# A recurrent-memory attention kernel: one output pass for regular and left rows, and attention scores in 12 products per head group with K's shared chunk in two half-zero planes

## The chip, the cores and the metric

The kernel runs on one core of a Trainium2 chip. The metric is the device time of one execution in microseconds (us); lower is better. Engine names as in the profile: PE is TensorE's matrix products and PEld its weight loads, DVE is VectorE, ACT is ScalarE, POOL is GpSimd, SP is the engine that issues most of the data transfers (DMAs).

## The reference, cut to what matters

```python
# B, S, Dm = 1, 2048, 640; H, Dh = 32, 192; M = 8 memory rows, seg_len = 32; Df = 1536; all bfloat16
mem = mem0
for s in range(S // seg_len):                    # 64 segments, one after the other
    h = concat([mem, x[s]])                      # 8 + 32 = 40 rows
    q, k, v = h @ Wq, h @ Wk, h @ Wv             # 32 heads of 192
    scores = where(mask, q @ k.T * Dh**-0.5, -1e9)
    o = (softmax(scores) @ v) @ Wo               # 40 x 640
    mem = o[:8]                                  # memory for the next segment
    outs.append(o[8:])
a = concat(outs)
b = (gelu(x @ w_gate) * (x @ w_up)) @ w_down
g = sigmoid((x * gate_w).sum(-1))
return g * a + (1 - g) * b
```

The next segment needs the 8 memory rows of this one, so the attention part is a chain of 64 steps.

## The kernel before

**Parts.** A feed-forward part comes first (the b branch, the gate, and x in a transposed form kept in DRAM). Then come 64 segments. A tile of 32 columns takes the 8 memory rows and the first 24 rows of x; they are called the regular rows. The last 8 rows of x are the left rows. Their Q, K and V do not depend on the memory, so these are computed for four segments at a time (4 x 8 = 32 rows, `left_mm`); Q and K of them are kept in DRAM as `left_qk_scratch`; they are read back into a stage and copied beside the regular columns by `left_fill`. q is the segment number modulo 4.

**Weights.** All weights together do not fit into SBUF. A piece is the [128, 1536] slice of Wq, Wk or Wv for 8 heads and one of five slices of Dm (384 KB), or a pair of heads of Wo (480 KB). Thirteen of the first and three of the second kind share their place with another piece: in every segment these 16 are replaced once used (`swap_loads`, `load_piece`, line 599, issued by SP in order), and are used again in the same segment for the last octet. An octet is 8 heads; a segment has four, and odd segments go through them backwards.

**Order of work.** `PROG` is a list written out by hand that gives the order of the items within a segment for all engines. `("g", n, k)` is slice k of a group of projections (`GROUPS`, up to three of Q, K, V sharing a stationary operand: lines 1046 and 226, 32-column tiles, four at once); `tq` and `tk` are the DVE transposes of Q and K (line 1080); `sc` the scores, `ex` the softmax, `pt` the transposed probabilities (lines 1144 and 1149), `pv` the products with V (lines 1177 and 1179), `wo` the products with Wo, two items per octet, `lf` and `le` products and read-out of the left Q and K (line 884, 891), `vb` V of the next left rows. There are seven groups: the last three are K of octet 3 behind V and Q, and V of octet 3 alone. Each engine takes its instructions in the order in which they are added; waits are set from the regions that an operation reads and writes.

**Scores (line 1083).** Scores of an octet go into one PSUM bank: two heads in the columns and four pairs. A head has 192 features, so a pair of heads has three chunks of 128: one of each head, and a middle one that holds 64 features of each. A mask product opens the bank (line 1087, two products), then eight products with all 128 rows (line 1095), then eight with 64 rows each for the middle chunk (line 1100, upper and lower half of the array). DVE then takes the maximum (1112) and subtracts it (1114), ACT the exponential (1124), DVE sum, reciprocal and the two products (1126 to 1131). Q and K, transposed, stand in `Qs` and `Ks`, 12 chunks of 40 columns.

**Products with V and Wo.** `pv_oct` writes the 40 columns per chunk and pair; ACT copies them into one of two buffers `uT` (line 1188; for octet 3 the third chunk is copied by DVE, line 1193). POOL copies the 8 left columns into `uTl` (line 1196), which gathers four segments. The 32 regular columns are multiplied by Wo at once: octets 0 to 2 in `wo_split` (line 1206, two head pairs side by side, four 32-column tiles of 320) with two halves that have to be added (`half_sums`: an ACT copy, line 1212, and two DVE sums, line 1215), octet 3 into a bank of its own (line 1229, 160 wide). The results are summed (line 1371) and transposed (line 1375) into the memory columns of the next segment; this is the boundary. In q3, `wo_left` takes the 32 gathered left rows through the same Wo pieces (also line 1206), behind each of the regular items and, for the last item, behind the boundary; `left_sums` adds their halves at the start of the next q0, after the first scores, reading bank 4.

**Small transfers.** Per four segments, `bzl_load` (line 952) reads the left rows of b in four DMAs and `outl_store` (line 961) writes the finished rows in four; both are issued by SP, the first in q2, the second in q0. The queue of SP is one list too: weight pieces, stages, the loads of b and the stores stand in program order.

Of the kernel before, what the change touches and what calls it, by code (L numbers as in the profile page):

```python
# [230 lines left out]

def _build(nc, A_x, A_mem0, A_Wq, A_Wk, A_Wv, A_Wo, seg_len, w_gate, w_up, w_down,
# [46 lines left out]
    total = int(nc.sbuf_bytes_remaining) - 64  # L279
# [5 lines left out]
    wsA = {}  # L285
    wsB = {}
    wsA["XB"] = al(DJ * 2)
    wsA["xs"] = al(KT * XA * 2)
    wsA["gall"] = al(NSEG * 4)
    wsA["gallL"] = al(32 * 4)  # L290
    wsA["ident"] = al(128 * 2)
    wsA["maskm"] = al(R * 2)
    wsA["elw"] = al(2 * 7 * 16 * 2)
    wsA["XLg"] = 2 * al(KT * 32 * 2)
    NVB, NUB = 2, 2
    wsB["bzl"] = al(DJ * 2)
    wsB["K"] = al(12 * R * 2)
# [5 lines left out]
    wsB["uT"] = al(NUB * 12 * R * 2)  # L303
    wsB["stats"] = al(2 * 3 * 4 * 4 + 8)
    wsB["p"] = al(4 * 64 * 2)
    wsB["uTl"] = al(NCH * 32 * 2)
# [63 lines left out]
    gallL = fview(wsA_off["gallL"], 128)  # L370
    r_gallL = sreg(wsA_off["gallL"], 128)
# [5 lines left out]
    elw = bview(wsA_off["elw"], 448).rearrange("p (i b r) -> p i b r", i=2, r=16)  # L377
    r_elw = sreg(wsA_off["elw"], 448)
# [5 lines left out]
    Ks = bview(wsB_off["K"], 12 * R * 2).rearrange("p (s r) -> p s r", r=R)  # L384
    r_Km = sreg(wsB_off["K"], 8)
    r_Kl = sreg(wsB_off["K"] + 8, 12 * R * 2 - 8)
    rows_sb = [bview(wsB_off["rows"] + b * 768, 768) for b in range(2)]
    r_rows = [sreg(wsB_off["rows"] + b * 768, 768) for b in range(2)]
    stg_off = (wsB_off["stg"], wsB_off["uT"] + 24 * R)
    assert 8 * LW <= 24 * R  # L390
# [23 lines left out]
    r_uTp = [[sreg(wsB_off["uT"] + b * UB, 4), sreg(wsB_off["uT"] + b * UB + 4, 4)] for b in range(NUB)]  # L414
    st_f = [[fview(wsB_off["stats"] + (3 * b + i) * 16, 16) for i in range(3)] for b in range(2)]
    r_st = [sreg(wsB_off["stats"] + 48 * b, 48) for b in range(2)]
    uTl = bview(wsB_off["uTl"], NCH * 64).rearrange("p (c t) -> p c t", t=32)
    r_uTl = [sreg(wsB_off["uTl"] + 12 * 64 * b, 12 * 64) for b in range(NOCT)]
    bz, bzl = [bview(wsB_off[nm], DJ * 2) for nm in ("bz", "bzl")]
    Zt = PT[:, 0:DJ]  # L420
    r_bzlj = [sreg(wsB_off["bzl"], DJ * 2, 32 * j, 32 * j + 32) for j in range(4)]
# [8 lines left out]
    fp_sz = {"xst": 16 * KT * XA * 2, "xls": 4 * KT * 64, "gr": 512 + 4 * NSEG + 128, "gwT": 64}  # L430
# [13 lines left out]
    r_gin = [sreg(o_gr + 512, 4 * NSEG, 32 * j, 32 * j + 32) for j in range(4)]  # L444
# [46 lines left out]
    def piece_src(key):  # L491
        if key[0] == 3:
            return Wo2[:, key[1]]
        m, o_, k = key
        return (Wq2, Wk2, Wv2)[m][:, k, OW * o_:OW * (o_ + 1)]
# [975 lines left out]
```

## Time and profile before

| what | value |
|---|---|
| runs of the kernel | 1756.74, 1765.19, 3865.19 us; median 1765.19 |
| span of the profiled execution | 1765.1 us |
| PE busy | 92% of the span |
| PEld, DVE, ACT, POOL busy | 46%, 54%, 45%, 18% |
| DMA engines busy with the main queue | 78.3% |
| moved | 499.57 MB, 283 GB/s on average |
| mean granted TensorE clock | 0.994 |
| start of segment 1 (first transpose of line 1375) | 204.3 us |

The profiled execution took 1765.1 us from its first to its last instruction, the median of the runs. Times in the profile are in us unless marked ns. A row with "x" and a count is a group of instructions; two numbers "start, us" in a timeline are the start and the length of a merged stretch, so what a product costs in a stream is read from one start to the next. In a list of waits the first name waited for the second. "issue" as the releaser means that the profile shows nothing that the engine waited for.

### The profile page before, as it was taken

The page shows a single profiled execution, that of the slowest core. Times are in us where ns is not written, and L with a number is a line of the kernel's source. Part 1 is how long each engine was busy: PE and PEld are TensorE (multiplying, and loading weights), DVE is VectorE, ACT ScalarE, POOL GpSimd, SP SyncE. Part 2 cuts the span into 40 slices and gives each one's busy share as a digit, 9 for nine tenths or more (in the row PEclk, how much of TensorE's full clock was granted, in tenths as well). Part 3 has the DMA queues.
Part 4 walks back from the last instruction along what each step waited for, and adds up shares of the span by engine and source line. Part 5 has one row for each costly group of instructions (what it writes and reads, how often), then busy time and mean ns, then how long its engine had stood idle before and what let it go on. Part 6 is the DMA issues. An engine that isn't in the chain of part 4 may idle for free.

```text
span 1765.1 us, 80301 instructions
## 1 busy us (share of the span) xinstructions
PE 1623.9 (92%) x39162; PEld 809.5 (46%) x31501; DVE 960.0 (54%) x2932; ACT 802.8 (45%) x1835; POOL 320.0 (18%) x1099
## 2 busy tenths in 40 slices
PE   9999999999999999999999989999999998999887
PEld 4554444444444444454444444454444444454444
DVE  2222655556555655555555655555555655655554
ACT  3222544545444544444444544444444544445443
POOL 1100111111112112111212111111211121121211
PEclk9999999999999999999999999999999999999999
DMA  9814987888778887888788887879787886879776
GB/s 335 295 48 157 329 313 250 320 313 288 280 269 311 299 308 253 315 290 319 281 280 293 296 293 250 314 285 323 279 280 275 311 310 241 312 282 327 283 275 238
DMA packets 271311, 499.57 MB, mean 283 GB/s; under 512 B 105304, under 2 KB 132208, under 8 KB 270960
## 3 DMA queue, kind: packets, MB, share of 16 engines
q1 hardware_dynamic: 267832, 491.34, 78.3%
q8 instruction: 276, 4.52, 1.0%
q10 hardware_dynamic: 3128, 3.09, 0.6%
q14 instruction: 75, 0.61, 0.1%
HBM read 473.22 MB, written 21.11 MB: 280 GB/s over the span
## 4 chain that ended last, share of the span: by engine, by line
PE 71%; DVE 15%; DMA 6%; issue 4%; ACT 4%; DVEq 0%; SPq 0%; ACTq 0%
PE ps L1046 20%; PE ps L226 15%; PE ps L1206 8%; DMA arena<-in_A_Wo_dram 5%; PE ps L1177 3%; PE ps L804 3%; PE ps L801 3%; PE ps L884 3%; PE ps L1100 3%; PE ps L819 2%; PE ps L1087 2%; DVE ps L1114 2%; DVE arena L1112 2%; PE ps L1095 2%; PE ps L1229 2%
## 5 line engine op out<-in xcount | busy, mean ns | idle before, releaser
L1046 PE MATMUL ps<-arena 128*32 128x384 bf16 x9940 | 723.0, 329 | 42.4 <-DVE arena L1375 34.4
L226 PE MATMUL ps<-arena 128*32 128x384 bf16 x7680 | 595.4, 328 | 7.9 <-DVE arena L1215 3.5
L1046 PEld LDWEIGHTS ps<-arena 128*32 128x32 bf16 x9940 | 257.5, 97 | 365.3 <-issue 226.0
L1080 DVE STREAM_TRANSPOSE arena<-arena 128x384 bf16<-128x384 bf16 x512 | 270.8, 557 | 150.8 <-ACT arena L1066 149.2
L1066 ACT ACTIVATE arena<-ps 128x384 bf16<-128x384 f32 x512 | 236.2, 489 | 211.6 <-PE ps L1046 196.3
L1206 PE MATMUL ps<-arena 128*32 128x320 bf16 x6144 | 293.6, 301 | 13.9 <-issue 13.4
L1124 ACT ACTIVATE ps<-ps 104x160 f32<-104x160 f32 x256 | 71.9, 281 | 293.4 <-DVE ps L1114 293.4
L1206 PEld LDWEIGHTS ps<-arena 128*32 128x32 bf16 x6144 | 163.5, 97 | 74.0 <-issue 19.4
L1112 DVE TENSOR_REDUCE arena<-ps 104x4 f32<-104x160 f32 x256 | 83.0, 324 | 165.8 <-PE ps L1100 164.6
L941 POOL COPY arena<-arena 128x96 bf16<-128x96 bf16 x256 | 70.3, 275 | 513.4 <-PE ps L1100 444.2
L1188 ACT ACTIVATE arena<-ps 128x480 bf16<-128x480 f32 (+1 forms) x256 | 137.0, 535 | 43.8 <-PE ps L1179 39.6
L1196 POOL COPY arena<-arena 128x96 bf16<-128x96 bf16 x256 | 68.3, 267 | 441.1 <-ACT arena L1188 357.3
L1162 ACT ACTIVATE arena<-ps 128x448 bf16<-128x448 f32 x192 | 104.2, 543 | 96.7 <-PE ps L1149 96.4
L1069 ACT ACTIVATE arena<-ps 128x384 bf16<-128x384 f32 x256 | 125.1, 489 | 20.9 <-PE ps L1046 16.3
L1177 PE MATMUL ps<-arena 128*64 128x160 bf16 x1536 | 123.1, 243 | 12.5 <-ACT arena L1162 6.9
L1126 DVE TENSOR_REDUCE arena<-ps 104x4 f32<-104x160 f32 x256 | 83.0, 324 | 92.5 <-ACT ps L1124 92.5
L1177 PEld LDWEIGHTS ps<-arena 128*64 128x64 bf16 x1536 | 80.8, 109 | 91.6 <-issue 31.7
L884 PE MATMUL ps<-arena 128*32 128x384 bf16 x1280 | 111.4, 330 | 2.2 <-issue 2.0
L1179 PE MATMUL ps<-arena 128*64 128x64 bf16 x1536 | 104.8, 193 | 4.1 <-issue 4.1
L891 DVE STREAM_TRANSPOSE arena<-arena 128x384 bf16<-128x384 bf16 x128 | 73.7, 576 | 31.6 <-ACT arena L889 27.8
L1215 DVE TENSOR_TENSOR arena<-ps,arena 64x160 f32<-64x160 f32 x160 | 50.8, 317 | 72.3 <-ACT arena L1212 61.6
L1114 DVE TENSOR_TENSOR ps<-ps,arena 104x160 f32<-104x160 f32 x256 | 85.0, 332 | 8.8
(84 smaller groups left out, 1819.2 us busy)
## 6 DMA issues: line engine op xcount, KB each, us to landing
arena<-in_A_Wk_dram SPq DMA_DIRECT2D x335, 384.0 KB, 7.1
arena<-in_A_Wv_dram SPq DMA_DIRECT2D x335, 384.0 KB, 9.1
arena<-in_A_Wo_dram SPq DMA_DIRECT2D x205, 480.0 KB, 6.4
arena<-in_A_Wq_dram SPq DMA_DIRECT2D x209, 384.0 KB, 5.4
arena<-left_qk_scratch SPq DMA_DIRECT2D x126, 96.0 KB, 2.8
left_qk_scratch<-arena SPq DMA_DIRECT2D x49, 192.0 KB, 2.3
left_qk_scratch<-arena SPq DMA_DIRECT2D x30, 96.0 KB, 5.7
ffn_b_scratch<-arena ACTq DMA_DIRECT2D x16, 160.0 KB, 4.4
```

The source lines that it names most:

```text
L226: return e.add_instruction(mybir.InstMatmult(name=nm, start_tensor_calc=like["start"], stop_tensor_calc=stop, tile_size=(128, 32), tile_po ...
L884: fns.append(lambda e, outp=outp, rhs=rhs, j=j: e.matmul(outp, lhs, rhs, start=(k == 0), stop=(k == KT - 1), tile_position=(0, 32 * j)))
L1046: fns.append(lambda e, outp=outp, rhs=rhs, j=j: e.matmul(outp, lhs, rhs, start=(k == 0), stop=(k == KT - 1), tile_position=(0, 32 * j)))
L1066: S_.add("act", lambda e, m=m, bk=bk: e.activation(out=rows_sb[m], in_=ps[:, bk, 0:384], func=ACTF.Copy), reads=[r_ps[bk]], writes=[r_rows ...
L1069: S_.add("act", lambda e, i=i, bk=bk: e.activation(out=v_sb[i % NVB].rearrange("p (c n) -> p c n", c=3), in_=ps[:, bk, 0:384].rearrange("p ...
L1080: S_.add("dve", lambda e: e.transpose(out=dst[:, :, 0:L], in_=rows_sb[m].rearrange("p (c r) -> p c r", r=L)), reads=[r_rows[m]], writes=[r ...
L1112: S_.add("dve", lambda e: e.tensor_reduce(out=mxs, in_=S3, axis=AX.X, op=ALU.max), reads=[rb], writes=[rst], name="smax max")
L1114: S_.add("dve", lambda e: e.tensor_tensor(out=S3, in0=S3, in1=mxb, op=ALU.subtract), reads=[rb, rst], writes=[rb], name="smax sub")
L1177: return [lambda e: e.matmul(full, v[:, e0:e0 + 64], PTm[:, i], start=True, stop=False, tile_position=(0, 64 * i), skip_group_check=True), ...
L1179: lambda e: e.matmul(part, vl[:, e0:e0 + 64], PTl[:, i], start=False, stop=True, tile_position=(0, 64 * i), skip_group_check=True)]
L1188: S_.add("act", lambda e: e.activation(out=apx(u[:, 0, 0, :], [[R, na], [3 * R, 4], [1, R]]), in_=ps[:, A, 0:na * W].rearrange("p (c t r) ...
L1206: fns.append(lambda e, i=i, t=t, j=j, gv=gv: e.matmul(ps[32 * j:32 * j + 32, bank, 0:2 * DJ].rearrange("p (h n) -> p h n", h=2), lhs2[i], ...
```

## The change

1. **Scores in 12 products.** K's two outer chunks go to one buffer (`KSA`). The middle chunk goes to two planes of another (`KSB`): the upper 64 rows into plane 0, the lower 64 into plane 1, and the other half of each plane is zero, set once. One product of all 128 rows and 80 columns then gives both heads of a pair: eight outer products and four middle ones (`score_mm`, `scores_mid`, item `sd`). K's DVE transpose becomes three: 128x256 and two of 64x128; POOL's copy of the left K becomes three likewise (`KPART`). Heads are paired anew (head h with h + 4), so V's products read two runs of 192 columns, and a Wo piece is put together from two heads' 64 rows.
2. **The joined output pass.** In q3 the octet's `uT` buffer is one of 64 columns (`U3`): 40 from the products with V, 24 from `uTl` by POOL. `wo_both` multiplies all 64 by a Wo piece, two products of 320 columns per chunk, into bank 4. `wo_left` is gone. The regular 32 rows are read out by two DVE and two ACT copies of 32x160 before the boundary's transposes; the left ones by four DVE operations in `left_sums`, with no halves to add.
3. **Order.** Six groups in place of seven, K before Q; `PROG` is written anew for q0 to q2 and `PROG3` for q3. The ACT copy of the half sums stays behind the last `wo` of octet 2; the DVE sums move behind the last `pv`.
4. **Small transfers.** The left rows are kept in the order of the new buffer (the fourth segment's first), so `bzl_load` and `outl_store` issue eight DMAs in place of four. Buffers in SBUF are packed anew to make room.

```diff
-    GROUPS = [[(0, 0), (1, 0)], [(2, 0), (0, 1), (1, 1)], [(2, 1), (0, 2)], [(1, 2)], [(2, 2), (0, 3)], [(1, 3)], [(2, 3)]]
+    GROUPS = [[(1, 0), (0, 0)], [(1, 1), (0, 1), (2, 0)], [(1, 2), (0, 2), (2, 1)], [(0, 3), (2, 2)], [(1, 3)], [(2, 3)]]
...
+    PROG = [("g", 0, 0), ("g", 0, 1), ("g", 0, 2), ("g", 0, 3), ("g", 0, 4), ("g", 1, 0), ("tk", 0), ("tq", 0),
+            ("g", 1, 1), ("g", 1, 2), ("sc", 0), ("sd", 0), ("g", 1, 3), ("ex", 0), ("g", 1, 4), ("g", 2, 0),
+            ("g", 2, 1), ("tk", 1), ("g", 2, 2), ("pt", 0), ("g", 2, 3), ("tq", 1), ("g", 2, 4), ("sc", 1),
+            ("sd", 1), ("lf", 2, 1, 0), ("pv", 0), ("g", 3, 0), ("g", 3, 1), ("tq", 2), ("g", 3, 2), ("lf", 1, 0, 0),
+            ("ex", 1), ("lf", 1, 0, 1), ("g", 3, 3), ("lf", 2, 1, 1), ("pt", 1), ("tk", 2), ("g", 3, 4), ("sc", 2),
...
+            ("lf", 0, 1, 2), ("pv", 3), ("lf", 1, 1, 4), ("le", 1, 1, 0), ("lf", 0, 1, 3), ("lf", 0, 1, 4),
+            ("le", 2, 1, 0), ("le", 2, 1, 1), ("le", 0, 1, 0), ("le", 1, 1, 1), ("wo", 3, 0), ("le", 0, 1, 1),
+            ("wo", 3, 1)]
+    PROG3 = [("g", 0, 0), ("g", 0, 1), ("g", 0, 2), ("g", 0, 3), ("g", 0, 4), ("tq", 0), ("g", 1, 0), ("g", 1, 1),
+            ("g", 1, 2), ("tk", 0), ("g", 1, 3), ("g", 1, 4), ("sc", 0), ("sd", 0), ("tk", 1), ("tq", 1), ("ex", 0),
...
+            ("g", 4, 3), ("tq", 3), ("g", 4, 4), ("wo", 0, 1), ("pv", 1), ("g", 5, 0), ("pt", 2), ("tk", 3),
+            ("sc", 3), ("sd", 3), ("wo", 1, 0), ("ex", 3), ("wo", 1, 1), ("pv", 2), ("g", 5, 1), ("g", 5, 2),
+            ("pt", 3), ("g", 5, 3), ("wo", 2, 0), ("g", 5, 4), ("wo", 2, 1), ("pv", 3), ("vb", 0), ("vb", 1),
+            ("vb", 2), ("wo", 3, 0), ("wo", 3, 1), ("vb", 3), ("vb", 4)]
...
+        for lo, hi, dst, cs, n in KPART:
+            S_.add("dve", lambda e, lo=lo, hi=hi, dst=dst, cs=cs: e.transpose(
+                out=dst[lo:hi, :, :, 0:L], in_=kparts(rows_sb[1], cs, L)[lo:hi]),
+                reads=[r_rows[1]], writes=[r_Km[n]], name="Tk%s s%d o%d" % ("b" if n else "", s, o))
...
-        for tl in range(4):
-            for gp in (0, 64):
-                fns.append(lambda e, gp=gp, c=3 * tl + 1, tl=tl: e.matmul(
-                    ps[gp:gp + R, bank, SC + tl * R:SC + (tl + 1) * R], Qs[gp:gp + 64, c, :], Ks[gp:gp + 64, c, :], start=False,
-                    stop=True, tile_position=(gp, gp), skip_group_check=True))
...
+        lo = SC + 2 * R * (t % 2) + (R if c == 2 else 0)
+        rhs, n = (KSB[:, t], 2) if c == 1 else (KSA[:, t, c // 2:c // 2 + 1], 1)
+        return lambda e: e.matmul(
+            ps[64 * (t // 2):64 * (t // 2) + R, bank, lo:lo + n * R].rearrange("p (x r) -> p x r", r=R), Qs[:, 3 * t + c, :], rhs,
+            start=False, stop=c == 1, tile_position=(0, 64 * (t // 2)), skip_group_check=True)
...
+    def wo_both(s, item):
+        for p in wo_pairs(s, item):
+            g_, rg_ = piece(s, (3, p))
             for c in range(3):
+                S_.add("pe", [lambda e, i=i, g_=g_, c=c, p=p: e.matmul(
+                    ps[64 * i:64 * i + 64, LB, 0:2 * DJ], U3[:, p % 4, c, :], g_[:, c, 2 * DJ * i:2 * DJ * (i + 1)],
+                    start=(p == NWP - 1 and c == 0), stop=(p == 0 and c == 2), tile_position=(0, 64 * i),
+                    skip_group_check=True) for i in range(2)],
+                    reads=[rg_, r_U3], writes=[r_ps[LB]], name="Wb s%d p%d" % (s, p))
...
+        if q == 3:
+            for j in (0, 2, 1, 3):
+                dst, src = Zt[32 * j:32 * j + 32], ps[64 * (j // 2):64 * (j // 2) + 32, LB, DJ * (j % 2):DJ * (j % 2 + 1)]
...
+            for n, (lo, hi) in enumerate(LROW):
+                S_.add(AUXQ, lambda e, j=j, n=n, lo=lo, hi=hi: e.dma_start(
+                    bzl[32 * j + M * n:32 * j + M * (n + hi - lo)], rows(b_scr, g)[1][lo:hi, :, DJ * j:DJ * (j + 1)]),
+                    reads=[Rg("dr", 128 * g, 128 * g + 128)], writes=[r_bzlj[j][n]], dma_sem="bzl%d" % (2 * j + n), name="bzl load g%d" % g)
```

## The prediction

> **What bounds the kernel now.** I read the page first.
> ```profile
> span 1765.1 us, 80301 instructions
> ...
> PE 1623.9 (92%) x39162; PEld 809.5 (46%) x31501; DVE 960.0 (54%) x2932; ACT 802.8 (45%) x1835; POOL 320.0 (18%) x1099
> ...
> q1 hardware_dynamic: 267832, 491.34, 78.3%
> q8 instruction: 276, 4.52, 1.0%
> ```
> TensorE is busy 92% of the span, and the weight stream keeps the DMA engines busy for 78%: two limits close together. The rest is asked by segment. The transposes of line 1375 hand the memory on, so I count a segment from the first of such a pair to the next. Segment 0 starts at 204 us after the feed-forward part, and 63 more follow. Let q be the number modulo 4. Mean lengths are q0 25.0, q1 25.0, q2 23.4, q3 25.3 us: 98.7 us per four, 15.75 fours. One four, by windows (busy us and instruction counts of PE, PEld, DVE, ACT, POOL, then clock, DMA share, GB/s; rows q1, q2, q3, q0):
> ```profile
> 601.65:626.92 25.27, 23.02 (x596) 10.84 (x452) 15.00 (x46) 12.28 (x29) 4.48 (x16) 1.00 0.88 306
> 626.92:650.46 23.54, 21.59 (x556) 10.19 (x432) 13.51 (x44) 11.54 (x27) 4.49 (x16) 1.00 0.87 303
> 650.46:674.55 24.09, 23.16 (x632) 12.38 (x528) 12.48 (x42) 11.07 (x26) 5.41 (x18) 1.00 0.79 291
> 674.55:699.90 25.35, 23.26 (x616) 11.80 (x492) 16.26 (x50) 12.18 (x28) 4.55 (x16) 1.00 0.78 274
> ```
> The two limits differ by segment: q1 and q2 run DMA at 0.87 to 0.88. A 384 KB weight piece lands every 0.97 us once the stream runs, a Wo piece every 1.2 us. The first piece is issued 0.85 us into a segment (1.9 us in q1) and lands at about 4.8 (q1: 5.9); the last Wo piece lands at 24.5, 22.3, 21.3 and 23.2 us in these four. From there some 0.8 us remain to the next segment (twelve products 0.4, sum and latency 0.4). So the weights alone ask for about 25.3, 23.1, 22.1 and 24.0 us. q2 stands 0.3 us above that, q3 3 us.
>
> What PE waits for (us in total, times, longest):
> ```profile
> PE ps L1046 <- DVE arena L1375: 34.4, 48, 1.2
> PE ps L1144 <- DVE arena L1131: 25.0, 65, 0.7
> PE ps L1206 <- issue: 13.4, 14, 2.0
> PE ps L1177 <- ACT arena L1162: 6.9, 15, 0.5
> PE ps L1229 <- DMA arena<-in_A_Wo_dram: 6.1, 10, 2.3
> ```
> The segment boundary costs about 0.7 us at 48 of 63 (after a q3 the late Wo pass hides it, 0.1). "Issue" waits sum to 35.6 us over all PE lines, 1.36 us per q3: up to 2 us in the middle of a group, where the instruction stream is densest. 4.52 MB over 276 fetches is 16 KB or 256 PE instructions each, so I read them as instruction fetch.
>
> **The scores.** PE's timeline of one head group:
> ```profile
> 1002.02 0.34 PE L226 MATMUL ps<-arena 128*32 128x384 bf16 x4
> 1002.28 0.25 PE L1087 MATMUL ps<-arena 128*40 128x160 bf16 x2
> 1002.37 0.26 PE L1095 MATMUL ps<-arena 128*40 128x40 bf16 x8
> 1002.56 0.27 PE L1100 MATMUL ps<-arena 64*40 64x40 bf16 x8
> 1002.76 0.35 PE L884 MATMUL ps<-arena 128*32 128x384 bf16 x4
> ```
> The starts are what count. Four 384-wide products take 0.16 us, yet 0.26 passes before the mask: 0.10 for entering the 64-column arrangement. Leaving costs the same (V's products: 0.12 to the next start, where a pair takes 0.03). Inside, L1095 to L1100 is 0.11 where a pair takes 0.03: again a change. The Trainium skill, TensorEngine Tiling (Array Packing), Key Properties, says that changing the mode, not just the tile, drains the engine. The trace agrees, at 0.08 to 0.10 us.
>
> Mask to exit is now 0.48 us. After: 0.09 mask, 0.11 for eight full products, two pairs of 128x80 half-zero products, 0.11 exit. A 128x80 pair is bounded by L1095's pair (0.029) and the 64x160 pair (0.07); I take 0.041, by its 80 columns. Sum 0.35: **-0.13 us** (-0.06 to -0.15) per head group, -0.52 per segment.
>
> Arrangement changes: scores and V's products now adjoin more often (two more places in q0 and q1, one in q2; each saves an exit and an entry, 0.2): -0.4, -0.4, -0.2. That rule also speaks against the joined pass, whose 64-column products stand among 32-column ones in q3: four more changes net, +0.4.
>
> **The joined pass (q3).** Streaming: before 42 fours of 320 columns at 0.134 and twelve of 160 at 0.071, 6.5 us; after 48 pairs of 320 at 0.135, 6.5 us. No gain by columns (the 64x160 row would allow +0.8). It halves the instructions, so I take 1.0 of the 1.36 us of issue waits off (0 to 1.3). It loses the filler behind the last Wo product: two copies of 0.31 on DVE (row L1193) and a transpose of 0.25 before PE resumes, with 0.33 us of vb products left: +0.65. U3's copy on POOL (between 0.28 and 0.69 us) lies beside groups and V's products; uncovered it would add 0.5 in each of three places.
>
> **K in three transposes.** 128x384 takes 0.557, 128x96 0.292, 128x64 0.249: by the line between, 128x256 is 0.43 and 64x128 0.31 (bounds 0.25 to 0.56). Neighbours overlap by some 0.06, so K costs 0.87 in place of 0.5. Where does it land? In q0 to q2 the first scores already wait for the first K transpose: rows at 2.55 us, two transposes to 3.62, products at 3.68. The new order runs three for K, one for Q: **+0.37**. In q3 two groups stand between: 0. In the second head group the scores now end at about 8.3 us with V's products right behind. Subtraction is done at 9.15, but ScalarE has K, Q, V and the 0.57 uT copy in its queue (starts 0.4 apart) and reaches the exponential at 9.65; sum, reciprocal and both products (0.33, 0.18, 0.29, 0.18 with their gaps) end at 11.0, where PE stands since 10.8. The third K, begun at 10.9, ends at 11.85, 0.1 after PE wants it: +0.3 in q1, and I take the same in q2. Later ones are covered by groups and left products. K's three POOL copies (about 0.7 for 0.27) start behind the scores, 3 us before they are needed: 0. V's weights read as two runs of 192 cost nothing either: Q's are read in twelve runs of 32 at the same 0.16. Wo's pieces keep rows of 3840 bytes: 0.
>
> **What the new order takes away.** The third softmax is now 4 us ahead of its transposes: of the L1131 and L1162 waits (0.48 in q0, 0.69 in q1, 0.73 in q2, 0.31 in q3) I take off 0.3, 0.6, 0.5, 0.3. The half sums move behind the last V products, so that their DVE copy no longer queues behind two 0.32 us sums: -0.3 in q1.
>
> **What is added in q0.** Four sums of 0.32 us read bank 4 before the third Q may write it (before: 0.4 us waited here): +0.5. A left transpose of 0.57 now precedes the final sum on DVE: +0.5.
>
> **SP's queue.** Gate-side loads and stores go from four to eight:
> ```profile
> 640.93 0.56 SPq L947 DMA_DIRECT2D arena<-ffn_b_scratch  x1
> 641.53 2.55 SPq L952 DMA_DIRECT2D arena<-ffn_b_scratch  x4
> 646.89 0.39 SPq L895 DMA_DIRECT2D left_qk_scratch<-arena  x1
> 647.38 0.45 SPq L935 DMA_DIRECT2D arena<-left_qk_scratch  x1
> 647.88 0.45 SPq L599 DMA_DIRECT2D arena<-in_A_Wk_dram  x1
> ```
> Four more issues are +2.6 us of SP in q2 and q0. SP stood free from 644.1 to 646.9 here; in a shorter q2 q3's first weight goes out about 1.1 us later, and q3's last K group, now needed at 11 to 12.7 us, waits: +0.6. In q0 the left store moves ahead of the boundary and no longer delays q1's weights, which start at 0.9 instead of 1.9 us and keep ahead of a faster q1 except at V's last group: +0.5, and the Wo wait (-0.35) goes.
>
> **Sums.** q0: -0.52-0.4+0.37-0.3-0.15 (issue)+0.5+0.5 = 0.0. q1: -0.52-0.4+0.37+0.3-0.6-0.15-0.3-0.35+0.5 = -1.15. q2: -0.52-0.2+0.37+0.3-0.5 = -0.55, held by the stream at 23.1, -0.35. q3: -0.52+0.4-1.0-0.3+0.65+0.6 = -0.17. Together -1.67 x 15.75 = **-26 us**: 1765.1 to **1739 us**, 1.5%. The span is the runs' median (1765.19), nothing to convert. I call no change what stays within 2%, 1729.9 to 1800.5.
>
> **Rivals.** (a) The weights keep up and hold nothing. Then q2 loses its 0.2, q3 and q1 their 0.6 and 0.5, q0's two additions are covered (1.0), and the second group's waits (0.6 in q1 and q2) as well: -2.9 more, -72 us, 1693. For: q3 has 3 us of slack. Against: q1 and q2 at 0.87.
> (b) Slower: the doubled small issues make the first weights late. It decides once the first piece leaves more than 2 us into a segment. If all 2.6 us reach q1 and q3, that is +2.6 and +1.5 more, 65 us. And waits near 2 us slow the clock: the 2.27 us wait for Wo at 1014 us was followed by 6.8 us at 0.50, and three pairs of waits summing to 1.5 to 1.75 us in the last segments by 3.4 us at 0.50 each. One such stretch per four loses 1.7 us, 27 us. 1739 + 92 = 1831; half of it 1785; I price it between, at 1808. The Trainium skill, TensorE: Matmul & The Clock Gate, Part 1, lets the clock fall after an idle window of about 3.4 us. Here partly idle ones did; by the page's wording the 27 us would go, and (b) would be near 1788.
> (c) The change doesn't do what it says: the scores gain 0.06 instead of 0.13 (+1.1 per four), as if a half-zero product cost what V's 64x160 does, and q3's fetch waits stay (+1.0): +33 us, 1772.
>
> Chances: forecast 0.40 (own range 1712 to 1765, a third of it beyond 2%), (a) 0.21, (b) 0.26 (a sixth of it within 2%), (c) 0.13. So faster 0.34, same 0.44, slower 0.22. The range runs from just below (a) to the lower half of (b), and takes in the bounds of the products: **1688 to 1795**.
>
> **What would show it.** Right: no 64*40 row; mask to next group near 0.35 us; issue waits near 20 us in total; a boundary of about 0.7 us after q3 too; K's 128x256 rows near 0.43. Wrong: PE waits on Wk or Wv rows above 20 us, a clock below 0.99, or U3's copy among PE's releasers.

## The result: almost twice the time

The changed kernel takes 3386.9 us (median of 4 runs, 3384.5 to 3387.8) where the kernel before takes 1764.4: a ratio of 1.925, 95% interval 1.920 to 1.930. The prediction said 1739 us with a range of 1688 to 1795, so it was wrong in sign and in size. One run of the kernel before, of 3865.2 us, was a slow one; the ratio is taken without it.

The page of the changed kernel, to be held against the lines shown of before:

```profile
span 3385.9 us, 74107 instructions
...
PE 1767.1 (52%) x36218; PEld 785.2 (23%) x27277; DVE 1067.1 (32%) x3430; ACT 785.6 (23%) x1835; POOL 432.4 (13%) x1614
...
PEclk9975677767767777777777767776777677777776
...
q1 hardware_dynamic: 265860, 491.33, 41.1%
q8 instruction: 248, 4.06, 0.5%
```

TensorE has 2944 instructions fewer and is busy 52% instead of 92%. The main queue moves the same 491.33 MB and keeps the engines busy for 41% instead of 78%: in time that is 1392 us against 1382, so the packets (one carries one row, 3840 bytes of a Wo piece) are neither more nor slower. What is new is that the engines stand still for more of the time, and the granted clock falls to 0.744 on average, from 0.994.

What TensorE waits for (us in total, times, longest):

```profile
PE ps L1290 <- DMA arena<-in_A_Wo_dram: 1096.2, 144, 9.2
PE ps L1308 <- DMA arena<-in_A_Wo_dram: 330.9, 48, 9.0
PE ps L1089 <- ACT arena L1112: 42.4, 1, 42.4
PE ps L1089 <- DVE arena L1462: 35.3, 63, 0.7
```

Lines 1290 and 1308 are the products of the output projection, in q0 to q2 and in the joined pass of q3. Before, this wait was 6.1 us in all (line 1229). Now it is 1427 us on these two lines, three times in each segment, whatever form the pass has. TensorE's timeline at the end of one segment (start, length, group, and in brackets the idle time before it):

```profile
1516.15 0.59 PE L1290 MATMUL ps<-arena 128*32 128x160 bf16 x12 [5.97 <-DMA arena<-in_A_Wo_dram]
1525.56 0.59 PE L1290 MATMUL ps<-arena 128*32 128x160 bf16 x12 [8.82 <-DMA arena<-in_A_Wo_dram]
1535.33 0.59 PE L1290 MATMUL ps<-arena 128*32 128x160 bf16 x12 [9.18 <-DMA arena<-in_A_Wo_dram]
1536.56 0.51 PE L1089 MATMUL ps<-arena 128*32 128x384 bf16 x4 [0.64 <-DVE arena L1462]
```

The starts stand 9.4 and 9.8 us apart: that is how fast Wo pieces land. Before it was one in 1.2 us. Three of the sixteen pieces are reloaded in each segment; 62 segments are 23.9 us longer each (1480 us), the first segment starts 115 us later, as thirteen Wo pieces are loaded during the feed-forward part, and the rest of the 1621 us lies behind the start of the last segment.

The packets of these pieces (3840 bytes, from the trace's packet records) still take 149 ns. But of the time in which any was on the way, exactly two were on the way in 93%; before, thirteen or more in about half of it. 64 packets in a row on each of two engines, 64 x 0.149 = 9.5 us, is the distance of the starts. (The trace doesn't name a packet's engine; that packets on the way stand for engines at work is a reading, which the runs with four and sixteen below bear out.) The diff has the reason in one line. With the new pairing of heads, a piece holds 64 rows of a head and 64 rows of the head four further on. Its source is therefore two runs far apart (a run of rows, here and below, is a stretch of them one behind the other in DRAM), where it was 128 rows one behind the other, and the transfer in the trace carries a destination of [1,128] elements of 3840 bytes, where it carried [128,1].

### The profile page after: what moved, and what is told of

Its sections match the earlier page's. It is cut to its first block, busy times and chain, and to the rows that moved or that the text cites. A ratio compares the mean times of both kernels' runs of the same rounds, so it can differ in the third digit from the quotient of the medians.

```text
span 3385.9 us, 74107 instructions
## 1 busy us (share of the span) xinstructions
PE 1767.1 (52%) x36218; PEld 785.2 (23%) x27277; DVE 1067.1 (32%) x3430; ACT 785.6 (23%) x1835; POOL 432.4 (13%) x1614
## 3 DMA queue, kind: packets, MB, share of 16 engines
q1 hardware_dynamic: 265860, 491.33, 41.1%
## 5 line engine op out<-in xcount | busy, mean ns | idle before, releaser
L226 PE MATMUL ps<-arena 128*32 128x384 bf16 x8960 | 720.9, 360 | 29.2 <-DVE arena L1357 17.9
L1290 PE MATMUL ps<-arena 128*32 128x160 bf16 x2304 | 107.5, 307 | 1106.6 <-DMA arena<-in_A_Wo_dram 1096.2
L1089 PEld LDWEIGHTS ps<-arena 128*32 128x32 bf16 x8660 | 244.7, 105 | 583.8 <-issue 353.3
L1290 PEld LDWEIGHTS ps<-arena 128*32 128x32 bf16 x2304 | 52.2, 114 | 1169.5 <-DMA arena<-in_A_Wo_dram 1136.4
L1308 PE MATMUL ps<-arena 128*64 128x320 bf16 x1536 | 148.7, 330 | 331.8 <-DMA arena<-in_A_Wo_dram 330.9
L1127 DVE STREAM_TRANSPOSE arena<-arena 64x128 bf16<-64x128 bf16 (+1 forms) x768 | 236.8, 334 | 146.3 <-ACT arena L1109 134.7
L1265 PE MATMUL ps<-arena 128*32 128x320 bf16 x3456 | 178.7, 301 | 10.3 <-DMA arena<-in_A_Wo_dram 9.1
L982 POOL COPY arena<-arena 64x32 bf16<-64x32 bf16 (+1 forms) x768 | 166.7, 217 | 47.3
L1123 DVE STREAM_TRANSPOSE arena<-arena 128x384 bf16<-128x384 bf16 x256 | 146.3, 572 | 55.4 <-ACT arena L1109 51.9
L979 POOL COPY arena<-arena 128x96 bf16<-128x96 bf16 x256 | 73.5, 287 | 651.4 <-PE ps L1146 463.1
L1161 DVE TENSOR_REDUCE arena<-ps 104x4 f32<-104x160 f32 x256 | 82.6, 323 | 102.7 <-PE ps L1146 102.7
L1146 PE MATMUL ps<-arena 128*40 128x40 bf16 (+1 forms) x3072 | 102.4, 188 | 18.9 <-DVE arena L1123 13.5
```

What stands on the lines that cost most here:

```text
L226: return e.add_instruction(mybir.InstMatmult(name=nm, start_tensor_calc=like["start"], stop_tensor_calc=stop, tile_size=(128, 32), tile_po ...
L982: S_.add("pool", lambda e, lo=lo, hi=hi, dst=dst, cs=cs: e.tensor_copy(out=dst[lo:hi, :, :, L:R], in_=kparts(stg[h][:, o % 2, 1], cs, M)[l ...
L1089: fns.append(lambda e, outp=outp, rhs=rhs, j=j: e.matmul(outp, lhs, rhs, start=(k == 0), stop=(k == KT - 1), tile_position=(0, 32 * j)))
L1123: S_.add("dve", lambda e: e.transpose(out=Qs[:, :, 0:L], in_=rows_sb[0].rearrange("p (c r) -> p c r", r=L)), reads=[r_rows[0]], writes=[r_ ...
L1127: S_.add("dve", lambda e, lo=lo, hi=hi, dst=dst, cs=cs: e.transpose(out=dst[lo:hi, :, :, 0:L], in_=kparts(rows_sb[1], cs, L)[lo:hi]), read ...
L1265: fns.append(lambda e, i=i, t=t, j=j, gv=gv: e.matmul(ps[32 * j:32 * j + 32, bank, 0:2 * DJ].rearrange("p (h n) -> p h n", h=2), lhs2[i], ...
```

## The experiments

Theory 1: the form of the Wo loads alone makes the loss, and the other steps of the prediction stand. Its rival: the new order, the third transpose for K or the doubled small transfers leave the stream too little room, and the slow pieces follow from that.

### The load form alone, in the kernel before

```diff
-    Wo2 = A_Wo.rearrange("h e n -> (h e) n").rearrange("(t p c) n -> p t c n", p=128, c=3)
+    Wo2 = A_Wo.rearrange("(o i t) (p c) n -> o t i p (c n)", i=2, t=4, c=3)
```

> The kernel before with nothing changed but the source of Wo's pieces: rows of heads h and h + 4 as in the changed kernel, one transfer with two runs of 64 rows. The output projection multiplies by the wrong head's rows for it; everything else is computed as before. Theory 1: three pieces of 9.5 us are issued from 13.4 us of a segment on, the last lands at about 44 us, so a segment takes 45 to 50 us, part of it at half clock: 3000 to 3400 us. Rival 2: the old order has room enough, the time stays near 1765 us, at most 1900.

Measured: 3364.7 us, ratio 1.907 (1.898 to 1.916). One changed view of the source gives all but 22 us of the loss, without a single instruction of the new order (this kernel multiplies by rows of the wrong heads; its work and bytes are those of before). The wait, in this kernel's list:

```profile
PE ps L1229 <- DMA arena<-in_A_Wo_dram: 1379.5, 192, 9.2
```

### How many engines carry a transfer

If two runs mean two engines, four must mean four, and sixteen all of them. In the same place:

```diff
# four runs
+    Wo2 = A_Wo.rearrange("(o i t) (h p c) n -> o t h i p (c n)", i=4, t=4, h=2, c=3)
# sixteen runs
+    Wo2 = A_Wo.rearrange("(o i) (h p c) n -> o h i p (c n)", i=16, h=8, c=3)
```

> The kernel before, with only the source of Wo's pieces changed: 32 rows from each of four heads, so one transfer of four runs of 32 rows of 3840 bytes (the output projection multiplies rows of the wrong heads; work and bytes are the same). Theory 1: as many DMA engines carry a transfer as it has runs. With two runs only two packets were ever on the way and a piece took 64 x 0.149 = 9.5 us; with four it takes 32 x 0.149 = 4.8 us, three pieces a segment save 14.3 of 48.2 us, the feed-forward part half of its 114 us: 261 + 63 x 33.9 + 43 = 2440 us (2250 to 2600), four Wo packets on the way. Rival: any source that is broken into runs far apart takes a slow path of two: 3360 as with two runs. A second rival: the length of a run costs nothing and two is an exception: 1765.

> The kernel before, with Wo's pieces taken as 8 rows from each of sixteen heads: one transfer of sixteen runs of 8 rows (wrong heads' rows again, the same work and bytes). Theory 1, as many engines as runs up to sixteen: back to the kernel before, 1765 us (1750 to 1790), Wo packets near 150 ns with up to 16 on the way. Rival: breaks in the source cost by themselves: above 2400.

Four runs: 2475.1 us (2440 expected), four packets on the way in 80% of the time, 149 ns each, and a longest wait of 5.2 us:

```profile
PE ps L1229 <- DMA arena<-in_A_Wo_dram: 566.1, 159, 5.2
```

Sixteen runs: 1906.6 us. Up to sixteen packets are on the way again, as theory 1 has it, but the time isn't the 1765 us that was expected: the packets' median is 246 ns in place of 149. So the number of runs sets how many packets are on the way, as if it set the number of engines, and something else made these packets slow. The Trainium skill, DMA: Bandwidth & Descriptors, section "Why a DMA increments its semaphore by 16 and not by 1", states the first half: a copy has an access pattern for its source and one for its destination (the dimensions that it walks through), and runs on the largest number of engines, at most 16, that divides the size of the slowest dimension longer than one in both of them. The traces agree, with 2, 4 and 16 packets on the way. By that rule alone the kernel with sixteen runs would be back at 1765.

### The changed kernel with each Wo piece in two loads

```diff
         if key[0] == 3:
+            for i in range(2):
+                S_.add("sp", ... e.dma_start(bview(res_off[key], GO, 64 * i, 64 * i + 64), piece_src(key)[i]), ...
```

> The changed kernel, but each piece of Wo is loaded by two transfers of 64 rows x 3840 bytes, one per head, in place of one transfer whose source is two runs of 64 rows. Theory 1: the whole loss comes from the form of that one transfer, which keeps two packets in flight (93% of the time that any 3840-byte packet is in flight) where the kernel before kept up to 16, so that a piece takes 64 x 0.149 = 9.5 us in place of 1.2. Then the waits for Wo (1096 + 331 us) shrink to under 30 us, the clock returns to 0.99, and the time is what the prediction's other terms give: near 1739 us, 1690 to 1795. Rival 2: the new order and the joined pass ask for Wo too soon after its place comes free (third wo item at 14 to 16 us, needed at 22 us). Then PE still waits several us for Wo in each segment, the clock stays under 0.9, and the time stays over 2000 us.

Measured: 1905.7 us, ratio 1.080 (1.076 to 1.084). Of the 1622 us that the change had added, 141 stay: the time lies between the 1739 of theory 1 and the 2000 and more of its rival. TensorE's waits:

```profile
PE ps L1095 <- DMA arena<-in_A_Wv_dram: 57.0, 76, 2.0
PE ps L1296 <- DMA arena<-in_A_Wo_dram: 51.3, 118, 2.3
PE ps L1095 <- DVE arena L1468: 40.3, 63, 0.7
```

Wo and V still come late, and here too the 3840-byte packets take 254 ns (median). Two parts of the change were taken out of this kernel, to see whether they are what is late.

Four small loads and stores of left rows in place of eight:

```diff
-            for n, (lo, hi) in enumerate(LROW):     # two transfers per quarter
+            S_.add(AUXQ, ... bzl[32 * j:32 * j + 32] ...)      # one, in load and store
```

> As the first, with the left rows of b read and the left output rows written by four transfers in place of eight (in plain row order, so the left rows are mixed with the wrong rows of b and gate). By the prediction's term for SP's queue the first weights of q3 leave 1.1 us earlier and 0.6 us per four segments go: 10 us less than the first. By its rival (b), if all of the eight issues stand on the path, 65 us less. If SP's queue has room, the same as the first within 4 us.

Measured: 1896.0 us, 10 below, which is the prediction's figure; but the intervals of the two ratios overlap (1.071 to 1.079 here, 1.076 to 1.084 with eight).

Without the two 64-row transposes of K's shared chunk:

```diff
-        for lo, hi, dst, cs, n in KPART:
+        for lo, hi, dst, cs, n in KPART[:1]:
```

> As the first, without the two 64-row transposes of K's shared chunk (its planes hold only the left keys, so the scores lack that chunk's regular keys). The prediction charges the three transposes with 0.37 us at the first scores of q0 to q2 and 0.3 us at the second of q1 and q2: 1.7 us per four segments, 27 us less than the first. If the order covers them, the same as the first within 5 us.

Measured: 1892.1 us, 14 below, half of the 27 expected. Neither makes the 141 us.

### The price of halves, in the kernel before

```diff
+            for i in range(2):
+                S_.add("sp", ... piece_view(key, res_off[key])[64 * i:64 * i + 64], piece_src(key)[64 * i:64 * i + 64] ...
```

> The kernel before, with each Wo piece loaded in two transfers of 64 partitions, everything else as it was; nothing is left out. Theory 1: a transfer that writes only half of the partitions is slow by itself (its 3840-byte packets took 251 ns in the changed kernel with halves, 162 in the kernel before): 128 packets a piece on 16 engines, 0.7 us more for each piece, 2.1 us a segment, of which q1 and q2 have no slack and q0 about 1: some 1845 us, with stretches at half clock up to 1890. Rival: a half costs only its second issue on SP (0.4 us, three a segment, beside other work): below 1785, and then the changed kernel with halves was slow for its new order.

Measured: 1883.0 us, ratio 1.070 (1.067 to 1.073), packets of 253 ns. Here the source is in one run, the work and its order are those of before, and still most of the loss with halves is there. The halves are slow by themselves; the rival with 1785 falls.

### Wo's rows put in order once, and whole loads

Where the form costs so much, it can be had otherwise: 32 copies of 64 rows, from DRAM to a scratch in DRAM, behind the first feed-forward block, where the DMA engines had little to do. Each later load of a piece is then 128 rows one behind the other.

```diff
+    wo_scr = nc.dram_tensor("wo_scratch", (NT, 128, 3 * Dm), BF, kind="Internal").ap()
-            return Wo2[key[1] // 4, key[1] % 4]
+            return wo_scr[key[1]]
+                    S_.add("sp", ... e.dma_start(wo_scr[p, 64 * i:64 * i + 64, :], Wo2[p // 4, p % 4, i]), ...
```

> The changed kernel, with Wo's rows brought once, during the feed-forward part, into the order in which the joined pass wants them: 32 copies of 64 rows from DRAM to a scratch in DRAM, issued after the first feed-forward block, where the DMA engines were busy 5 to 37% of the time. Each Wo piece in the segments is then one load of 128 whole rows of 3840 bytes, as in the kernel before. Nothing is left out. Theory 1: the load form was the only thing wrong, the other steps of the prediction hold: 1739 us, 1700 to 1785; Wo packets near 150 ns and never only two at a time, waits for Wo below 15 us, clock 0.99 or more. From the kernel with the halves it comes out alike: its 1904.6 us less the waits for Wo (51) and V (57) and about 55 us of half clock leave 1742. Theory 2: the new order itself asks for more than the weight stream or SP's queue can give, and the halves only showed it: V's waits stay above 40 us and the time is 1840 or more.

Measured: 1754.3 us, where the kernel before took 1760.6 beside it: ratio 0.9966 (0.9948 to 0.9983). Theory 1 holds for the load form: the whole loss is gone. For the other steps it holds in part, since the gain is 6 us where the prediction had 26. The page and the waits of this kernel:

```profile
span 1754.2 us, 74139 instructions
...
PE 1582.0 (90%) x36218; PEld 758.1 (43%) x27277; DVE 1061.0 (60%) x3430; ACT 783.4 (45%) x1835; POOL 426.6 (24%) x1614
...
q1 hardware_dynamic: 269754, 499.21, 81.0%
```

```profile
PE ps L1095 <- DVE arena L1468: 52.8, 63, 1.5
PE ps L1152 <- DVE arena L1129: 21.5, 48, 0.9
PE ps L226 <- DVE arena L1363: 17.9, 15, 1.2
PE ps L1271 <- issue: 14.7, 15, 1.5
PE ps L1296 <- ACT arena L1253: 10.3, 18, 0.6
PE ps L1095 <- DMA arena<-in_A_Wk_dram: 7.1, 17, 1.2
PE ps L1296 <- DMA arena<-wo_scratch: 5.1, 14, 0.9
```

Wo is down to 5.1 us, and the packets' median is 149 ns. What is left are mostly waits for DVE, ScalarE and instruction fetch: this is the kernel that the prediction had worked out, and its steps can be read from it (next section).

Two of them by experiment, on the same chip. Four small transfers, as above:

> As the kernel with the rearranged copy of Wo, and with the four small loads and four small stores of left rows of the kernel before in place of eight each (the left rows are then mixed with other tokens' rows; the work and the bytes are the same). Theory 1, the prediction's term for SP's queue (0.6 us in q3, 0.5 in q1): 17 us below the kernel with eight. With the halves it was 10. Rival: SP's queue has room again once a Wo piece is one issue, and the difference is under 4 us.

Measured: 1756.8 us, ratio 0.9972 (0.9952 to 0.9991). No gain: SP's queue has room, the rival holds.

Without the transposes of K's shared chunk. The edit took out one thing more than the expectation says: POOL's two copies per head group that bring the left rows into these planes went with the transposes (POOL runs 1102 instructions in place of 1614). So the planes hold zeros only, the scores lack that chunk's part from all keys, and the figure is that of transposes and copies together.

> As the kernel with the rearranged copy of Wo, without the two block transposes of 64 rows of K's shared chunk (the scores lack that chunk's part from the regular keys; the same products run on planes that hold only zeros and the memory's rows). Theory 1, the prediction's term (0.37 us in q0, q1, q2 and 0.3 more in q1 and q2): 27 us below the kernel that has them. Rival: the transposes lie mostly beside a weight stream that sets the time, as with the halves, where they were worth 14 us: 0 to 15 us.

Measured: 1731.2 us, 23 below the kernel that has them, ratio 0.9833 (0.9799 to 0.9866). By segment q0 -0.61, q1 -0.86, q2 -0.20, q3 +0.09 us. In sum that is near the 27 expected.

### The sums of left rows, earlier

In q0 the third Q waits 1.19 us for four sums that read bank 4.

```diff
-                if i == 0 and q == 0 and g > 0:
-                    left_sums(g - 1)          # behind the scores of the first head group
+        if q == 3:
+            left_sums(g)                      # at the end of q3, behind the mixing
```

> The kernel with the rearranged copy of Wo, with the four sums of left rows that read bank 4 (SCALAR_TENSOR_TENSOR on 32x160, 0.383 us each, 1.63 in a row) issued at the end of q3, right behind the mixing on VectorE, in place of behind the first softmax's two reads in q0. Nothing is left out. Theory 1: the third Q in q0 waits 1.19 us for these sums (17.9 us over 15); VectorE stands still for 1.68 us ahead of K's transposes there, so that the sums fit in for nothing: 0.95 to 1.2 us off each q0, 14 to 18 us, near 1738. Rival: the sums now end where K's transposes begin and push them; each 0.3 us of that comes back in the first scores: 1746. A second rival: something else of q0 (Wo's pass, fetch waits) takes the whole place of the wait: 1754 as before.

Measured: 1748.2 us, where the kernel before took 1766.2 beside it: ratio 0.9883 (0.9855 to 0.9911), against 0.9966 for the kernel without this edit. DVE's timeline shows the sums ending where K's transposes begin, with nothing pushed:

```profile
570.70 0.34 DVE L1025 SCALAR_TENSOR_TENSOR arena<-arena 128x160 bf16<-128x160 bf16 x1
571.07 1.63 DVE L1363 SCALAR_TENSOR_TENSOR arena<-ps,arena 32x160 bf16<-32x160 f32 x4
572.73 0.97 DVE L1133 STREAM_TRANSPOSE arena<-arena 128x256 bf16<-128x256 bf16 x3
```

The wait for line 1363 is gone from TensorE's list, and q0 falls from 25.77 to 25.06 us, which is short of the 0.95 to 1.2 expected. By the times, the two ratios stand apart by 15 us (on two chips, and each is known to some 3 to 5 us); 0.71 x 16 = 11 would be most of that. But in the profiled execution, the longest of its six with 1755.3 us, the other three segments are 0.14 to 0.25 us longer than with the late sums, and four together only 0.18 us shorter. There TensorE waits longer for V's weights in q2 (4.0 us in all, 0.9 before the edit) and for K's in q3 (9.7, 7.1 before). How much of q0's gain the weight stream takes back in the faster executions is not shown. This is the fastest version that does the whole work, about 1.2% below the kernel before, which is less than the 2% that I call a difference.

### One weight group ahead of the first scores

```diff
-            ("g", 1, 1), ("g", 1, 2), ("sc", 0), ("sd", 0), ("g", 1, 3), ("ex", 0), ("g", 1, 4), ("g", 2, 0),
+            ("g", 1, 1), ("g", 1, 2), ("g", 1, 3), ("sc", 0), ("sd", 0), ("ex", 0), ("g", 1, 4), ("g", 2, 0),
```

> As the kernel with the early sums, and in q0, q1 and q2 one more weight group stands ahead of the first scores (the group that stood right behind them), so that TensorE has 0.5 us of products while VectorE runs three transposes for K and one for Q. Nothing is left out. Theory 1: the first scores wait 0.45 us for Q's transpose 48 times (21.5 us); most of that goes, the scores themselves come 0.1 us later: 12 to 21 us below the kernel with the early sums. Rival: q2 stands at what the weight stream asks (23.07 us, and 23.1 was worked out), and in q1 and q0 the first softmax, later by the same amount, gives the wait back at the bank that the second Q group needs: below 5 us.

Measured: 1753.3 us, ratio 0.992 (0.9895 to 0.9945): no gain over the early sums, the rival holds. The 21.7 us of waits for Q's transpose (line 1129) are gone from the list, and these stand in it instead:

```profile
PE ps L226 <- ACT arena L1115: 18.5, 32, 0.6
...
PE ps L1095 <- ACT arena L1115: 12.0, 15, 0.8
```

With the early sums alone the second of them was 4.6 us, and the first did not occur. Line 1115 is ScalarE's copy of K and Q out of the banks. The products that came earlier only meet the next bank earlier; the pace there is that of the copies.

### Why packets take 250 ns on sixteen engines

> The kernel before, with each Wo piece loaded in four transfers of 32 partitions; nothing is left out. The question is why a 3840-byte packet takes 253 ns (median) in transfers of 64 partitions and 247 in sixteen runs of 8 rows, on 16 engines, where one transfer of 128 rows shows 149. Theory 1: at any time those forms write through half of the ways into SBUF, two engines on each; partitions 0 to 31 already use the same half as 0 to 63, so quarters show the same 250 ns as halves. The Trainium skill, DMA: Bandwidth & Descriptors, section The descriptor swizzle, gives such a map (engine by partition, 32 apart sharing a port). Theory 2: the rate goes with the number of partitions written: near 500 ns. Theory 3: short transfers are slow by their start and end: between, and higher the shorter. Time by theory 1: like the halves, 1885, and up to 40 more for six more issues a segment on SP.

> The kernel before, with each Wo piece loaded in two transfers of 64 partitions, the lower half issued by SP and the upper half by ScalarE's queue; nothing is left out. Theory 1 (half of the ways into SBUF per transfer): where the two halves run at the same time they use all ways, and packets fall back toward 149 ns: a median below 200. Theories 2 and 3 (partitions or the length of a transfer): each half keeps its 250 ns or more, since the two share the 16 engines. The time is not the point, as ScalarE's stream now waits for free slots: between 1765 and 1950.

The edits are that of the halves, with 32 rows four times, and with the second half on ScalarE's queue. Quarters: 1917.7 us, packets 241 ns, as theory 1 has it and far from 500. Two queues: 1946 us, and here theory 1 falls: packets keep 244 ns, and those that start while five or more of the other queue are on the way take 245, on either queue. The packets by how many are on the way as one starts, itself among them (median ns; 1 to 4, 9 to 12, 13 to 16; all in the order of the kernel before):

```
whole loads              149   149   149
halves                   155   255   256
quarters                 154   248   244
sixteen runs             154   233   245
halves, two queues       152   242   247
```

So the 250 ns comes with many packets side by side, and is not a price of a short transfer; of these forms, one transfer of 128 rows one behind the other is the only one in which sixteen go side by side at 149. The 3072-byte packets of the other weights, which are whole loads of 128 rows in all of these kernels, keep their 121 ns (median) throughout, so it is not the memory or the engines as a whole that became slower. What the slow packets share stays open. Of the Trainium skill's page DMA: Bandwidth & Descriptors, the section "The descriptor swizzle" gives the 128-partition transfer one way into SBUF per engine, and two engines on one way in the other forms would fit the halves, the quarters and the sixteen runs; that two halves at once didn't help speaks against the simple form of it.

## Why the prediction was wrong

**The step that failed** is the end of the part on K, and in it the last sentence: "V's weights read as two runs of 192 cost nothing either: Q's are read in twelve runs of 32 at the same 0.16. Wo's pieces keep rows of 3840 bytes: 0." The rows did keep their size and the packets their 149 ns. I priced a transfer by its rows and never asked on how many engines it runs. The part that moves Wo's rows was priced at 0 and measured, alone, at +1600 us in the kernel before. No rival contained it either: rival (b) had late weights, but through SP's queue, by 2.6 us, not through the transfer itself. Of the stated signs of being wrong the clock showed it (0.744); the waits that the signs named, for Wk and Wv, do not occur in the changed kernel's list, where Wo is late. The diff shows the source with a dimension of two in front, and the landing time of a Wo piece (1.2 us) stood in the text; a source in two runs had no row in the trace of before, and such an operation needs a bound from both sides. The upper one was at hand: the 128 packets of a piece one after the other, 128 x 0.149 = 19 us (an estimate from the packet's time in the trace of before). The rule of the Trainium skill named above speaks against this very load, and I had not weighed it.

**The other steps**, read from the kernel with whole loads (mean segment lengths in us, change against before; the prediction had 25.0 and 25.3 for q1 and q3 of before, where the trace has 25.06 and 25.21):

| | before | predicted | whole loads | early sums |
|---|---|---|---|---|
| q0 | 25.01 | 0.0 | +0.76 | +0.05 |
| q1 | 25.06 | -1.15 | -0.86 | -0.71 |
| q2 | 23.42 | -0.35 | -0.35 | -0.21 |
| q3 | 25.21 | -0.17 | -0.28 | -0.03 |
| sum | 98.70 | -1.67 | -0.73 | -0.90 |

1754 against the 1739 forecast: with the Wo step right, the forecast would have been 15 us too low, and 1754 lies inside its range; 12 of the 15 us are q0's (0.76 x 15.75). Measured by the gain it is further off: -0.73 us per four in place of -1.67, less than half.

- **Scores**: right. Mask to twelve products to the next thing is short, and the 64-row products are gone:

```profile
601.50 0.25 PE L1141 MATMUL ps<-arena 128*40 128x160 bf16 x2
602.22 0.35 PE L1152 MATMUL ps<-arena 128*40 128x40 bf16 x12 [0.47 <-DVE arena L1129]
602.50 0.35 PE L1095 MATMUL ps<-arena 128*32 128x384 bf16 x4
...
606.37 0.25 PE L1141 MATMUL ps<-arena 128*40 128x160 bf16 x2
606.46 0.34 PE L1152 MATMUL ps<-arena 128*40 128x40 bf16 x12
606.63 0.23 PE L1235 MATMUL ps<-arena 128*64 128x160 bf16 x2
```

  The second group has 0.09 for the mask and 0.17 for the products, 0.26 where V's products follow in the same arrangement (0.49 before); with 0.28 from the products to a 32-column group, as in the first, mask to exit is 0.37 (forecast 0.35, before 0.48).
- **K in three transposes**: right. The first scores wait 0.47 us here for Q's transpose (line 1129), 21.5 us in all over 48 segments, 0.45 each, where 0.1 to 0.16 passed before; the forecast added 0.37. The transposes, forecast at 0.43 and 0.31:

```profile
L1133 DVE STREAM_TRANSPOSE arena<-arena 64x128 bf16<-64x128 bf16 x512 | 145.5, 284 | 8.9
...
L1133 DVE STREAM_TRANSPOSE arena<-arena 128x256 bf16<-128x256 bf16 x256 | 111.2, 434 | 69.1 <-ACT arena L1115 66.5
```

  Taken out with their copies they were worth 23 us, forecast 27. By segment (q0 to q3) that is 0.61, 0.86, 0.20 and -0.09 us against 0.37, 0.67, 0.67 and 0: the sum is nearer than its parts.
- **The third softmax** (0.3, 0.6, 0.5 and 0.3 taken off): right. TensorE's waits for lines 1131, 1130 and 1162, 33.8 us before, are down to 4.4 us for the same steps (lines 1186 and 1185).
- **Fetch waits** ("I take 1.0 of the 1.36 us of issue waits off"): right in sum, 19.9 us in place of 33.9 (the prediction's 35.6 is a little too high). In q3 none is left of 1.35 us each. But 14.7 us now stand in q0, in nearly every one a wait of up to 1.5 us among its Wo products, about 21 us into the segment: q0 has 0.9 us of them where it had 0.35, and the sum took 0.15 off. That they are instruction fetch was only read from sizes; the trace bears it out. All 26 of these waits end 2.2 to 3.1 us after a 16 KB packet of the instruction queue q8 starts, and these packets start 6.2 us apart (median).
- **Bank 4 in q0** ("+0.5"): mis-sized. The sums take 0.383 us each and not 0.32, and they stand behind the first softmax's two steps: TensorE waits 1.19 us per q0 (17.9 us, 15 times) where it waited 0.23 (3.5 us, 15 times), +0.96. Moving them took the wait away.
- **The left transpose in front of the final sum of q0** ("+0.5"): right. DVE's two left transposes (line 930) now stand in front of the sum of line 1464, and TensorE waits for the memory columns. At the end of one q0:

```profile
694.50 1.09 PE L1296 MATMUL ps<-arena 128*32 128x160 bf16 x48
...
695.15 1.26 DVE L930 STREAM_TRANSPOSE arena<-arena 128x384 bf16<-128x384 bf16 x2 [0.17 <-ACT arena L928]
...
696.33 0.21 DVE L1464 TENSOR_TENSOR arena<-ps,arena 128x64 bf16<-128x64 f32 x1
...
696.88 0.35 PE L1095 MATMUL ps<-arena 128*32 128x384 bf16 x4 [1.29 <-DVE arena L1468]
```

  The wait behind a q0 is 1.18 us on average where it was 0.68. From the start of the last Wo product to the next segment q0 takes 1.11 us, before 0.61.
- **q2 held by the weight stream at 23.1** ("-0.35"): the figure came (23.07 us, -0.35), in part by luck. The waits for weights in q2 are 3.6 us in all, 0.22 each. Beside them stands a wait that the sum did not have: in every q2 Wo products of the last octet wait 0.57 us for ScalarE's copy of line 1253 (16 of the 18 such waits). And without K's transposes and copies q2 fell to 22.87 us.
- **SP's queue** (+0.6 in q3, +0.5 in q1): the cause was wrong. Eight small transfers or four are the same with whole loads; with halves, where the stream was late, the 10 us lie within the spread. The wait foreseen for q3's K weights is there, 7.1 us in all, 0.45 each, but with four small transfers it is 8.1. In q1 the waits for weights are 3.5 us in all, 0.22 each.
- **The joined pass** (q3, sum -0.17): near, -0.28. The boundary now costs 0.63 us behind a q3 too, where it was hidden (forecast 0.7, +0.65 in the sum). Against the other stated signs of being wrong, waits on K's and V's weights stay under 10 us, the clock is 0.994, and U3's copy (line 1249) holds TensorE for 1.1 us in all.

## What to carry to other kernels

Price a transfer by its bytes, its row size and also by how many of its packets go side by side; look in the access pattern for what stands in front. Here a rearranged source that put a 2 there kept two packets on the way, and nothing in the packets' size or time showed it: ask what the trace shows for that form, and where it shows none, bound it by one packet after the other. If rows must be taken from two places every time round a loop, put them in order once, in a scratch, and load them whole.

When products move ahead of a wait, look which copy or bank they meet next: the early group gained nothing, while sums that fitted into a stretch in which DVE stood still took a wait of 1.2 us away (ratio 0.988 against 0.997).

## What the runs showed of the hardware that I had not expected

- Transfers of 128 rows of 3840 bytes: two, four or sixteen runs in the source put 2, 4 or 16 packets on the way; by the packets' times that is 9.5, 4.8 and, with slower packets, about 2 us a piece (estimates: 64 x 0.149, 32 x 0.149, 8 x 0.246); the starts in the trace with two stood 9.4 and 9.8 us apart.
- The same packet takes 149 ns (median) in one transfer of 128 rows one behind the other, and 241 to 254 ns in halves, quarters or sixteen runs of 8 rows. With up to four on the way these forms take 152 to 155, with nine or more 233 and up. In the kernel before, halves alone cost 7%. The Trainium skill's page DMA: Bandwidth & Descriptors, section "Rules for kernel authors", advises one 128-partition transfer over two halves; the traces agree, and give the price.
- TensorE at half clock with waits: in the changed kernel, with three waits of 6 to 9 us in the segment shown, the granted clock was 0.50 from 1512 to 1536 us and 0.744 on average; with waits for weights of up to 2.3 us in the halves it was 0.971, and 0.994 with whole loads.
